# One transfer of 26 rows instead of four strided ones, when z is loaded for the last stage of an FFT convolution

## The chip, the cores and the metric

The kernel runs on one core of one Trainium2 chip. The metric is the device time of one execution in microseconds. The kernel before took 869.53 us as the median of three runs (863.26, 869.53 and 874.21). An execution by the hardware profiler took 871.26 us, of which the profile shows a span of 869.5 us.

The core has a matrix engine (TensorE, PE in the profile), three engines for element-wise work (VectorE or DVE, ScalarE or ACT, GpSimd or POOL) and SyncE (SP), which here does nothing but issue transfers. Data moves between the large memory (HBM) and the on-chip memory of 128 partitions (SBUF) by 16 DMA engines.

## The reference

The first half is a long convolution over the sequence, done by FFT; the second is a "soft mixture of experts" on its result. In short:

```python
# x: (8, 5696, 128), h: (5696, 128)
L = 2 * S
Xf = np.fft.rfft(x, n=L, axis=1)
Hf = np.fft.rfft(h, n=L, axis=0)
y = np.fft.irfft(Xf * Hf[None], n=L, axis=1)[:, :S, :]
x = y.reshape(B * S, D)                        # (45568, 128)

logits = x @ phi                               # 32 slots
d = np.exp(logits - logits.max(0));  d /= d.sum(0) + 1e-9
slot_input = (d.T @ x).reshape(8, 4, 128)
slot_out[e] = np.maximum(slot_input[e] @ w1[e], 0) @ w2[e]
c = np.exp(logits - logits.max(1, keepdims=True));  c /= c.sum(1, keepdims=True) + 1e-9
out = c @ slot_out
```

Everything is float32. All 8 batches pass through the convolution before the experts can run, since the softmax `d` goes over all 45,568 tokens.

## The kernel before

The convolution is a transform of length 5760 = 90 x 64 (`N1, N2 = 90, 64`), written as matrix products in stages. Between the stages the data goes through HBM, because the next stage needs it in another order:

- `load_x` (line 195) loads x into three buffers `xc`; `fold` (line 206, GpSimd) folds them; `first_low` and `first_high` (line 217, TensorE) do the transform over 89 rows, ScalarE copies the result out (line 220), and line 226 writes it to HBM as `f`.
- `load_g` (line 253) loads `f` into four buffers `gt`; `stage_b1` (lines 267 to 294) transforms over the 64 columns and multiplies by the filter; `stage_b2` (lines 309 to 318) transforms back and writes `z` to HBM.
- `load_pair` (line 346) loads a "pair" of column groups of `z` for all 90 rows; `stage_c1` (line 365) does the last transform over the 90 rows, lines 370 to 384 fold the result, and `stage_c2` to `stage_c6` and `dispatch` do logits, softmax terms and the sums for the slots.

There are 32 pairs, four for each batch. One step t of the main loop runs all stages for different parts of the data: the first stage of one piece, the middle of one a few steps older, the last of one older still. The order within a step is written out as two strings, `ORDER_O` and `ORDER_E`, one letter for each piece of work; a pair takes one step of each kind. `z`, the letter for `load_pair`, stands first in `ORDER_O`, and `1`, for `stage_c1`, stands in `ORDER_E`. Each engine runs its own instructions in the order in which they were written; nothing is reordered later.

SP issues nearly all transfers, in that order: about 32 for one pair. Every one of them uses one of eight completion semaphores, in turn, and waits before its issue until the transfer that used this semaphore last has landed; so no more than eight are on their way. It waits as well for the engine that makes its data or frees its buffer.

`load_pair` has one buffer `zc` (in the tail, after line 641, a second one, `zd`). It has 128 partitions of 16 KB; a row of the load, that is one of the 90 row numbers, fills one partition, 16 KB in one piece in HBM as well. Which row goes to which partition is said by `z_blocks` (lines 18 to 21), a list of (first row, rows, first partition, step of the partitions):

```python
left = [(64 + 8 * j, min(8, n - 64 - 8 * j), j, 4) for j in range((n - 57) // 8)]
return [(0, 64, 32, 1)] + left
```

For n = 90 these are rows 0 to 63 in partitions 32 to 95; rows 64 to 71 in partitions 0, 4, ..., 28; rows 72 to 79 in 1, 5, ..., 29; rows 80 to 87 in 2, 6, ..., 30; rows 88 and 89 in 3 and 7. Each entry is one transfer. Partitions 11, 15, 19, 23, 27 and 31, and those from 96 on, hold zeros. The table `i1` of the last transform, which line 365 multiplies with, is laid out by the same list, so that each row meets its own coefficients.

The tail begins after the main loop. There `zd` is taken into use and gets the six partitions of zeros below 96 by a copy from `zc` (line 653); with `zd` the matmuls read 96 partitions only (`used`).

Of the kernel before, what the change touches and what calls it, by code (L numbers as in the profile page):

```python
# [16 lines left out]

def z_blocks(n):

    left = [(64 + 8 * j, min(8, n - 64 - 8 * j), j, 4) for j in range((n - 57) // 8)]  # L20
    return [(0, 64, 32, 1)] + left


def transform_tables(S, N1, N2, CH, X0):
# [29 lines left out]
    for r, n, p, step in z_blocks(N1):  # L54
        i1[p:p + (n - 1) * step + 1:step, :, 0:NP] = part[r:r + n]
# [22 lines left out]
def kernel(  # L78
# [31 lines left out]
    N1, N2 = 90, 64  # L110
# [227 lines left out]
    def load_pair(T):  # L338
        if T >= NT:
            return  # L340
        b, j = divmod(T, NQ)
        t_ = zring.pop(0)
        zring.append(t_)
        w_ = 2 * 2 * CH * 2 * D
        for r, n, p, step in z_blocks(N1):
            nc.sync.dma_start(
                out=t_[p:p + (n - 1) * step + 1:step, :, :, :, :, :].rearrange("k h o n c d -> k (h o n c d)"),
                in_=zd[b].rearrange("q (a r) c d -> (q a) (r c d)",
                                    a=2)[r:r + n, j * w_:(j + 1) * w_])
        zs[T] = t_  # L350
# [293 lines left out]

    T = V + 1
    used = sum(z_blocks(N1)[0][1:3])
    held = slice(N1 // 64 * 8 + 3, used - 64, 4)
    front.close()
    rings.append(mid.enter_context(tc.tile_pool(name="ps2", bufs=4, space=PSUM)))
    last = work.enter_context(tc.tile_pool(name="last", bufs=1))  # L650
# [200 lines left out]
```

## Time and profile before

| | |
|---|---|
| median of three runs | 869.53 us |
| the profiled execution | 871.26 us |
| its span | 869.5 us |
| TensorE busy | 778.0 us, 89% |
| VectorE busy | 617.7 us, 71% |
| ScalarE busy | 438.1 us, 50% |
| GpSimd busy | 392.7 us, 45% |
| moved by the DMA engines | 272.01 MB, 313 GB/s on average |
| SP's transfers (queue q1) | 89.9% of 16 engines' span |
| mean granted TensorE clock | 0.939 |

"Busy" is the time in which an engine executed something. The page of the profile also follows back the chain of work that ended last, lists the groups of instructions with what ended the idle time before them, and lists the transfers by the line that issued them. Other views give the busy time in chosen stretches, the instructions in order of time, and who waited for whom. "SPq" is SP's queue of transfers; its entries say when a transfer was issued, not when it landed. The 4-byte packets in the DMA records are the writes to semaphores by which the DMA engines report that their share of a transfer is done.

### The profile page before, as it was taken

What the parts mean: (1) busy time and instruction counts of PE and PEld (TensorE: products, weight loads), DVE (VectorE), ACT (ScalarE), POOL (GpSimd) and SP (SyncE); (2) the same over time, 40 slices, a digit from 0 to 9 for tenths busy, and PEclk for the clock granted to TensorE, in tenths of its full rate; (3) what the DMA queues carried; (4) which work ended last, traced back from release to release, by engine and by line L of the source; (5) the groups of instructions that cost most, each with busy time, mean ns of one, the idle gap of its engine ahead of it and who ended that gap; (6) DMA issues with size and microseconds to landing.
All of it is one profiled execution on the core that took longest, in us unless ns stands there. A gap on an engine that the chain in (4) does not pass through costs nothing.

```text
span 869.5 us, 20507 instructions
## 1 busy us (share of the span) xinstructions
PE 778.0 (89%) x7796; PEld 378.0 (43%) x7796; DVE 617.7 (71%) x929; ACT 438.1 (50%) x967; POOL 392.7 (45%) x372
## 2 busy tenths in 40 slices
PE   5888788889999999999999999899987878978882
PEld 1122333234444444444444444444444544445882
DVE  3059867667778878887888777677888994963641
ACT  2433244354656566566556565555654444562541
POOL 4453433244565666666555556546444332541000
PEclk9999999999999999999999999999999897997755
DMA  9899899999999999999999999999988885760998
GB/s 300 267 293 320 291 332 349 326 347 330 334 320 351 334 339 331 338 350 321 328 343 341 327 329 338 329 326 342 332 279 279 319 311 206 270 263 3 371 381 325
DMA packets 153245, 272.01 MB, mean 313 GB/s; under 512 B 11878, under 2 KB 110054, under 8 KB 150005
## 3 DMA queue, kind: packets, MB, share of 16 engines
q1 hardware_dynamic: 152571, 270.38, 89.9%
q8 instruction: 63, 1.03, 0.5%
q10 hardware_dynamic: 576, 0.31, 0.1%
q14 instruction: 35, 0.29, 0.1%
HBM read 142.57 MB, written 127.98 MB: 311 GB/s over the span
## 4 chain that ended last, share of the span: by engine, by line
PE 62%; DVE 13%; DMA 12%; issue 3%; SPq 2%; ACT 1%; POOL 0%; DVEq 0%; ACTq 0%
PE bank L217 14%; PE bank L365 13%; PE bank L309 8%; PE bt L267 7%; PE bank L393 6%; DMA out_dram<-o 4%; DMA zc<-z 3%; PE bank L480 3%; DVE p L285 3%; DVE bt L285 3%; DVE yf L294 2%; PE bank L402 2%; PE bank L431 2%; DMA xc<-in_x_dram 2%; DMA gt<-f 2%
## 5 line engine op out<-in xcount | busy, mean ns | idle before, releaser
L206 POOL TENSOR_TENSOR x<-xc 128x512 f32<-128x512 f32 x144 | 180.0, 1273 | 229.8 <-PE bank L217 208.8
L217 PE MATMUL bank<-x,s 128*32 128x512 f32 (+1 forms) x1152 | 228.2, 614 | 15.5 <-POOL x L206 14.3
L315 ACT ACTIVATE zst<-bank 128x512 f32<-128x512 f32 (+1 forms) x184 | 98.6, 586 | 186.1 <-PE bank L309 165.5
L220 ACT ACTIVATE fst<-bank 128x512 f32<-128x512 f32 x216 | 127.5, 598 | 109.9 <-PE bank L217 90.3
L285 DVE TENSOR_TENSOR p<-bt,Hi 128x1024 f32<-128x1024 f32 x96 | 111.4, 1160 | 33.7 <-PE bt L267 32.9
L365 PE MATMUL bank<-zc,i 128*64 128x512 f32 x480 | 120.2, 624 | 9.2 <-DMA zc<-z 8.6
L309 PE MATMUL bank<-yf,vt 64*64 64x256 f32 x1440 | 102.9, 393 | 27.4 <-DVE yf L294 27.4
L217 PEld LDWEIGHTS bank<-x,s 128*32 128x32 f32 (+1 forms) x1152 | 56.5, 125 | 155.1 <-issue 75.8
L294 DVE TENSOR_TENSOR yf<-bt,p 128x512 f32<-128x512 f32 x192 | 119.4, 663 | 3.3
L267 PE MATMUL bt<-gt,wt 64*64 64x256 f32 x1620 | 113.7, 388 | 6.3 <-PE bt L267 2.3
L285 DVE TENSOR_TENSOR bt<-bt,Hr 128x1024 f32<-128x1024 f32 x96 | 113.0, 1177 | 0.0
L267 PEld LDWEIGHTS bt<-gt,wt 64*64 64x64 f32 x1620 | 54.0, 132 | 81.2 <-issue 38.3
L309 PEld LDWEIGHTS bank<-yf,vt 64*64 64x64 f32 x1440 | 57.0, 136 | 59.0 <-issue 31.0
L384 POOL TENSOR_TENSOR y<-y,op 128x512 f32<-128x512 f32 x64 | 77.9, 1218 | 8.7 <-DVE op L370 5.3
L370 DVE TENSOR_TENSOR y<-bank,y 128x512 f32<-128x512 f32 x32 | 22.1, 692 | 74.5 <-PE bank L365 74.2
L384 POOL TENSOR_TENSOR y<-y,om 128x512 f32<-128x512 f32 x54 | 64.0, 1185 | 2.1
L393 PE MATMUL bank<-ident,y 109*128 109x109 f32 x512 | 64.0, 277 | 0.7 <-DVE y L384 0.7
L365 PEld LDWEIGHTS bank<-zc,i 128*64 128x64 f32 x480 | 30.8, 139 | 73.3 <-issue 50.4
L393 PEld LDWEIGHTS bank<-ident,y 109*128 109x128 f32 x512 | 54.0, 150 | 16.6 <-issue 11.1
L395 ACT ACTIVATE yt<-bank 128x360 f32<-128x360 f32 x128 | 51.3, 490 | 2.9 <-PE bank L393 2.6
L804 PE MATMUL op<-so,cT 32*128 32x128 f32 x704 | 45.7, 379 | 6.0 <-ACT o L813 5.5
L439 POOL MEMSET dt<- 64x8 f32 x32 | 3.4, 106 | 101.4 <-issue 61.4
(95 smaller groups left out, 809.9 us busy)
## 6 DMA issues: line engine op xcount, KB each, us to landing
gt<-f SPq DMA_DIRECT2D x99, 512.0 KB
z<-zst SPq DMA_DIRECT2D x88, 512.0 KB
f<-fst SPq DMA_DIRECT2D x144, 240.0 KB
zc<-z SPq DMA_DIRECT2D x30, 1024.0 KB
xc<-in_x_dram SPq DMA_DIRECT2D x64, 320.0 KB
f<-fst SPq DMA_DIRECT2D x144, 120.0 KB
out_dram<-o SPq DMA_DIRECT2D x16, 1024.0 KB
zc<-z SPq DMA_DIRECT2D x90, 128.0 KB
```

The lines of the kernel that those rows point to most:

```text
L206: nc.gpsimd.tensor_tensor(out=y_[:, :, :], in0=t_[:, 0, :, :], in1=t_[:, 1, ::-1, :], op=AL.subtract if comp else AL.add)
L217: nc.tensor.matmul(p[o * width:(o + 1) * width, :], s1[:, comp + G, k], folded[(c, comp)][:, :, :].rearrange("p n d -> p (n d)"), start=Tr ...
L220: nc.scalar.activation(st[:, :, G, :], p[:, :].rearrange("p (n d) -> p n d", d=D), AF.Copy)
L267: nc.tensor.matmul(bt[q * HP:(q + 1) * HP, a, o, :], wt[r, 2 * i + q, :], t_[r, 2 * o + q, :, :].rearrange("p c d -> p (c d)"), start=True ...
L285: nc.vector.tensor_tensor(out=p_, in0=pv, in1=h_, op=AL.mult)
L294: eng.tensor_tensor(out=y_[r, 0:k, c, :], in0=pv[:, :, c, :], in1=pi[r, 0:k, 1 - c, :], op=op_)
L309: nc.tensor.matmul(bz[q][a * HP:(a + 1) * HP, o * 2 * D:(o + 1) * 2 * D], vt[r, i, a, :], y_[r, a * m + o, :, :].rearrange("p c d -> p (c ...
L315: nc.scalar.activation(st[:, 0:m, q, :], bz[q][:, 0:m * 2 * D].rearrange("p (o x) -> p o x", o=m), AF.Copy)
L365: nc.tensor.matmul(p[h_ * HP:(h_ + 1) * HP, :], i1[0:kr, tab, :], t_[0:kr, h_, o, :, q, :], start=True, stop=True)
L384: eng.tensor_tensor(out=part_, in0=part(v, 0), in1=o_[:, :, :], op=sign)
L393: nc.tensor.transpose(p[:, i * TR:(i + 1) * TR], ys[T][0:TR, k * CH + i, 0:D], ident[0:TR, 0:TR])
L395: nc.scalar.activation(yt[:, k * CH:(k + 1) * CH, :, :], of_tokens(p), AF.Copy)
```

## The change

Rows 64 to 89 come in a single transfer into partitions 0 to 25 instead of in four transfers into every fourth partition. The table `i1` follows by itself, and the partitions of zeros are now 26 to 31.

```diff
 def z_blocks(n):
 
-    left = [(64 + 8 * j, min(8, n - 64 - 8 * j), j, 4) for j in range((n - 57) // 8)]
-    return [(0, 64, 32, 1)] + left
+    return [(0, 64, 32, 1), (64, n - 64, 0, 1)]
...
     T = V + 1
     used = sum(z_blocks(N1)[0][1:3])
-    held = slice(N1 // 64 * 8 + 3, used - 64, 4)
+    held = slice(N1 - 64, used - 64)
```

`load_pair`, which loops over this list, stays as it is:

```python
for r, n, p, step in z_blocks(N1):
    nc.sync.dma_start(
        out=t_[p:p + (n - 1) * step + 1:step, ...].rearrange("k h o n c d -> k (h o n c d)"),
        in_=zd[b].rearrange(...)[r:r + n, j * w_:(j + 1) * w_])
```

So a load has two transfers, of 1 MB and 416 KB, in place of five. The bytes, their places in HBM and the matmuls that read them are the same.

## The prediction

> **What bounds the kernel now.** I read the page first, then the busy time by stretch, the DMA queue's timeline and waits, and last the DMA packet records.
>
> The page's chain of waits, one group of matmuls (busy us, mean ns, idle before and its releaser), and its DMA issues:
>
> ```profile
> PE 62%; DVE 13%; DMA 12%; issue 3%; SPq 2%; ACT 1%; POOL 0%; DVEq 0%; ACTq 0%
> ...
> L365 PE MATMUL bank<-zc,i 128*64 128x512 f32 x480 | 120.2, 624 | 9.2 <-DMA zc<-z 8.6
> ...
> zc<-z SPq DMA_DIRECT2D x30, 1024.0 KB
> ...
> zc<-z SPq DMA_DIRECT2D x90, 128.0 KB
> ...
> zc<-z SPq DMA_DIRECT2D x30, 32.0 KB
> ```
>
> TensorE carries the chain, but the only thing that the matmuls reading zc ever visibly waited for is the transfer that the change touches: 8.6 us over the run. The last three lines are that load: per pair T one transfer of 64 rows, three of 8 and one of 2, a row being 16 KB.
>
> Busy time by stretch (us busy and count per engine, granted clock, DMA share, GB/s):
>
> ```profile
> 180.00:260.00 80.00, 77.05 (x768) 34.55 (x764) 61.61 (x92) 45.00 (x96) 44.43 (x41) 0.98 0.97 334
> ...
> 340.00:420.00 80.00, 79.27 (x822) 36.92 (x820) 64.94 (x100) 48.01 (x110) 46.50 (x45) 1.00 0.97 336
> ...
> 500.00:580.00 80.00, 76.43 (x772) 35.94 (x768) 60.14 (x94) 45.93 (x106) 47.31 (x44) 0.98 0.97 332
> ...
> 720.00:780.00 60.00, 53.18 (x445) 28.78 (x444) 42.29 (x75) 33.33 (x89) 26.35 (x31) 0.89 0.70 264
> ```
>
> From 180 to 640 us two resources are full at once: PE 79.27 of 80 us, and the 16 DMA engines 0.97. In the chain the same matmuls return every 20.26 us (L217 at 335.17, 355.43, 375.69), which is one pair. From 720 us on the DMA share is 0.70.
>
> The DMA queue over half a pair, and its waits between 260 and 640 us (total us, times, longest):
>
> ```profile
> 329.11 0.35 SPq L318 DMA_DIRECT2D z<-zst  x1
> 329.56 3.23 SPq L346 DMA_DIRECT2D zc<-z  x5
> 332.84 1.50 SPq L253 DMA_DIRECT2D gt<-f  x3
> 335.09 0.82 SPq L195 DMA_DIRECT2D xc<-in_x_dram  x2
> 336.02 0.78 SPq L226 DMA_DIRECT2D f<-fst  x2
> ...
> SPq L195 <- DMA gt<-f: 35.9, 25, 2.0
> SPq L195 <- DMA zc<-z: 19.2, 23, 2.5
> SPq L226 <- DMA z<-zst: 16.7, 24, 1.0
> SPq L318 <- DMA gt<-f: 16.3, 17, 1.9
> ```
>
> SP mostly waits for earlier transfers: [...]SP is held by how fast transfers finish, not by its own issue time.
>
> The packet records of the trace, those of 16,384 bytes (only zc's rows have them in numbers), give the load itself. A packet takes 611 ns at its median in the quiet rounds (608 at least). In the load issued at 329.56 the 64-row transfer runs from 330.9 to about 334.1 as four rounds of 16; then come rounds of 8, 8, 8 and 2 that start near 334.1, 334.7, 335.3 and 336.0; the last ends at 336.71. TensorE first reads it at 338.82: 2.1 us to spare. Over the 27 loads of the main loop up to 690 us this spare time is 0.55 to 3.75 us; in ten it is under 0.9 us, and 0.55 to 0.63 is the least there is. There the landing itself released TensorE.
>
> [...] So 64 rows use 16 engines, 8 use 8, 2 use 2, and 26 will use 13. [...] q1 has 11,558 packets of 4 bytes. The rounds of 8 agree too.
>
> [...] Here a lone packet runs at 16,384 B / 611 ns = 26.8 GB/s[...].
>
> [...]
>
> **The change part by part.**
>
> *Issue.* 32 loads (30 into zc, 2 into the second buffer zd) issue 2 transfers in place of 5: 96 fewer of 0.602 us (median of L346), 58 us of SP time, 1.8 us a load. It is hidden work: SP waits on transfers behind it (L195 alone 35.9 + 19.2 us in 19 pairs, about 2.9 us a pair). What follows (the three gt transfers, xc, f) may wait for an older transfer than before, since three places of the ring of eight fall away. I take 0; at best it is worth part of C and D below.
>
> *Engines.* Before, the 26 rows cost engines 0 and 1 four packets (2.44 us), 2 to 7 three (1.83), 8 to 15 none. After, 13 engines take two each. [...] Lower bound, no mutual hindrance: 2 x 0.611 = 1.22 us, landing 1.2 us earlier. Upper bound, shared halves: [...] 2.44 us, the landing as before, but with 13 engines held for 2.44 us where 26 packets' worth of work is done. I take the upper one[...]. Added engine time: 26 x 0.611 = 15.9 us a load.
>
> *What of it reaches the end.* A pair has 16 x 20.26 = 324 us of engine time, and the share of 0.97 leaves 0.03 x 324 = 9.7 free. The overflow is 15.9 - 9.7 = 6.2 us, over 16 engines 0.39 us a pair. Through the 23 pairs from 180 to 640 us: 8.9 us. Later loads (share 0.84, then 0.70) have room: 0. The spare time before TensorE absorbs it at first but doesn't refill, as SP, the landing and TensorE go round together. Next late are the zc landing, then gt behind it[...].
>
> *Waits.* On the first load of a batch the last z rows must have landed. Before, only the 2-row transfer waited for that, at the end; now the 26-row one does, second, with gt, xc and f behind it on SP. The z transfer is issued 0.45 us before the load, so this can hold SP about 2 us, eight times; but the 64-row transfer occupies the engines for 3.2 us meanwhile. I take 0, at most 8 us.
>
> *Once.* The copy of the six zero rows into the second buffer (L653, issued at 724.15) goes from six spread partitions to 26 to 31[...]. 0. The reordered rows of the table i1 and the same 128-row matmuls cost nothing: the other engines' instructions stay as they are.
>
> Sum: + 8.9 us. The profiled execution took 871.26 us (span 869.5), 1.7 over the median of 869.53; on the median that is **878 us**.
>
> **The rivals.**
>
> A, as above: 878, from 872 (half the overflow fits elsewhere) to 886.
>
> B, slower by over 2%: the DMA engines have nothing free. 0.97 is a mean that counts overlapped packets, and a transfer is done only when its slowest engine is. Then the whole 15.9 / 16 = 0.99 us a load comes through in 30 loads: 869.5 + 30 = 899. For it: the spare time runs down inside the loop (1.83, 1.29, 1.42, 0.55, 0.86, 0.63, 0.55 in the loads issued from 411 to 533 us), so the transfers fall behind TensorE already. Against it: that time recovers after 575 us, and the tail has room. It decides once a load lands more than about 0.9 us later, which is what ten loads have at most.
>
> C, no cost: the landing is set by the four packets of engine 0 before[...]; a transfer waits for its slowest engine anyway, so engines 8 to 12 merely lose idle time. SP's 1.8 us a load helps a little: 863 to 871, say 868.
>
> D, faster: [...] loads land 1.2 us earlier, and the ten loads without spare time save about 1.1 each: 869.5 - 11 = 858. Over 2% (17 us) would need the transfers to bound most pairs, which PE at 79 of 80 us speaks against.
>
> That the change doesn't do what it says is ruled out by the built program: 26-row transfers, 96 DMAs fewer.
>
> **How the numbers follow.** A 0.36, B 0.32, C 0.24, D 0.08. About 2% is what a measurement of this kernel can tell from no change: 852 and 887 are the bounds. Slower by over 2%: B and the top of A, 0.36. Faster: the end of D, 0.04. The rest 0.60. The range is from 861 (just under C, leaving out most of D) to 902 (B with its waits).
>
> **What would show it.** Right: q1's 4-byte packets fall to 11,142; zc's last 26 packets take about 1.2 us each rather than 0.61, and the landing comes no earlier after the issue (7 to 9 us now); the DMA share rises above 0.97; L365 waits longer than 8.6 us for zc. B: the same with over 25 us of such waits or pairs of over 21 us. C: long packets, yet pairs of 20.26 us. D: packets of 0.61 us and landings 1.2 us earlier. A changed time outside 168 to 770 us would prove the whole account wrong.

## The result, and the profile after

The changed kernel takes 902.98 us as the median of four runs (900.52 to 905.14), the kernel before 868.38 us beside it (863.26 to 874.21): a ratio of 1.0388, 95% interval 1.0338 to 1.0438. It is slower by 34.6 us, clearly more than the 2% of the prediction's bound, and 1 us above the upper end of its range (861 to 902).

The page after gives the chain of waits, and the group of matmuls that reads zc (busy us, mean ns, idle before it and who ended it):

```profile
PE 49%; DMA 28%; DVE 11%; issue 3%; ACT 1%; SPq 1%; POOL 1%; DVEq 0%; ACTq 0%
PE bank L364 13%; DMA zc<-z 13%; PE bank L216 10%; PE bank L308 6%; PE bt L266 6%; DMA out_dram<-o 5%; PE bank L392 4%; DMA gt<-f 4%; DMA xc<-in_x_dram 4%; DVE p L284 2%; DVE bt L284 2%; DVE yf L293 2%; PE bank L479 2%; PE bank L430 2%; DMA f<-fst 2%
...
L364 PE MATMUL bank<-zc,i 128*64 128x512 f32 x480 | 128.9, 662 | 34.2 <-DMA zc<-z 28.6
```

The line numbers are one lower than before. Part of the chain has moved from TensorE (62% before, 49% now) to the DMA engines (12% before, 28% now). The group waits 34.2 us where it waited 9.2, and its matmuls themselves take 128.9 us in place of 120.2. Together that is 25.0 + 8.7 = 33.7 us, close to the 32.3 by which the profiled span grew (869.5 to 901.8).

The busy time of the main loop, first before and then after (us, five engines busy, granted clock, DMA share, GB/s):

```profile
260.00:640.00 380.00, 373.20 (x3838) 174.48 (x3840) 303.69 (x465) 225.62 (x516) 219.09 (x204) 1.00 0.97 334
```

```profile
260.00:640.00 380.00, 362.01 (x3608) 165.14 (x3600) 286.55 (x441) 215.39 (x489) 208.90 (x194) 0.98 1.01 317
```

The DMA engines are busier, 1.01 against 0.97, and yet move less, 317 GB/s against 334. A share above 1 also says that the records of one engine overlap, so the share isn't a fraction of something that ends at 1.

The DMA queue after, in a stretch like that shown of before, and its longest waits between 260 and 640 us (total us, times, longest):

```profile
342.62 0.35 SPq L317 DMA_DIRECT2D z<-zst  x1
343.06 2.59 SPq L345 DMA_DIRECT2D zc<-z  x2
345.71 1.48 SPq L252 DMA_DIRECT2D gt<-f  x3
347.27 1.09 SPq L194 DMA_DIRECT2D xc<-in_x_dram  x2
348.42 1.19 SPq L225 DMA_DIRECT2D f<-fst  x2
...
SPq L194 <- DMA gt<-f: 37.7, 27, 2.6
SPq L317 <- DMA zc<-z: 33.4, 18, 3.0
SPq L225 <- DMA z<-zst: 23.3, 31, 1.2
SPq L317 <- DMA gt<-f: 21.4, 18, 2.2
SPq L225 <- DMA zc<-z: 12.3, 12, 2.1
```

A load is two issues now, and in this stretch SP is through with it only a little earlier (2.59 us in place of 3.23). What it saves it loses further on: the transfers that come eight places after the load's wait 33.4 + 12.3 = 45.7 us for it, 26.0 before (19.2 + 5.4 + 1.4). In the records of after, 744 of 745 of SP's transfers use the semaphore of the one eight places before, and each is issued after that one's last write to it. (SP issues fewer transfers than the description of the kernel says: 92 from 340 to 420 us before, which is 23 for a pair and not 32.)

The starts of the zc matmuls, load by load, tell where the time went: the first is 2.5 us late (178.74 against 176.25), the 17th 27.4 us (528.24 against 500.81), the 23rd 27.5 (654.16 against 626.67), the 27th 32.8 (733.03 against 700.20). What comes after adds nothing. Between the 17th and the 23rd load nothing is lost either: there the kernel before itself took 21.0 us a pair.

In the packet records zc's 16,384-byte packets between 168 and 690 us have a mean of 852 ns (714 before), and 906 of them took over 800 ns (436 before). The packets of the 64 rows hardly changed (median 646 ns, 644 before); those of the 26 rows have a median of 1,188 ns (611 before). From the start of its first packet to the end of its last, a load takes 7.21 us on average (6.36 before). q1 has 11,142 packets of 4 bytes, 416 fewer than the 11,558 of before. That is 13 for each of 32 loads: 8 + 8 + 8 + 2 = 26 writes before, 13 after, read as 13 engines with two rows each. The records don't name the engine of a packet; engine numbers, as in the recorded texts, are the author's labels, read from rounds such as those of 8, 8, 8 and 2.

### The profile page after: what moved, and what is told of

It is laid out like the page before. It is cut to its first block, busy times and chain, and to the rows that moved or that the text cites. A ratio compares the mean times of both kernels' runs of the same rounds, so it can differ in the third digit from the quotient of the medians.

```text
span 901.8 us, 20351 instructions
## 1 busy us (share of the span) xinstructions
PE 784.9 (87%) x7796; PEld 379.0 (42%) x7796; DVE 617.6 (68%) x929; ACT 437.7 (49%) x967; POOL 392.6 (44%) x372
## 4 chain that ended last, share of the span: by engine, by line
PE 49%; DMA 28%; DVE 11%; issue 3%; ACT 1%; SPq 1%; POOL 1%; DVEq 0%; ACTq 0%
PE bank L364 13%; DMA zc<-z 13%; PE bank L216 10%; PE bank L308 6%; PE bt L266 6%; DMA out_dram<-o 5%; PE bank L392 4%; DMA gt<-f 4%; DMA xc<-in_x_dram 4%; DVE p L284 2%; DVE bt L284 2%; DVE yf L293 2%; PE bank L479 2%; PE bank L430 2%; DMA f<-fst 2%
## 5 line engine op out<-in xcount | busy, mean ns | idle before, releaser
L364 PE MATMUL bank<-zc,i 128*64 128x512 f32 x480 | 128.9, 662 | 34.2 <-DMA zc<-z 28.6
L364 PEld LDWEIGHTS bank<-zc,i 128*64 128x64 f32 x480 | 33.7, 147 | 101.8 <-issue 72.5
```

Source lines behind the costliest of these rows:

```text
L364: nc.tensor.matmul(p[h_ * HP:(h_ + 1) * HP, :], i1[0:kr, tab, :], t_[0:kr, h_, o, :, q, :], start=True, stop=True)
```

## The experiments

Theory P is the author's assumption behind the upper bound of the prediction, which no view of before showed: engines that write at the same time to partitions close together (neighbours, or every second one) halve each other, called sharing below; an engine that takes four neighbouring partitions by itself is not held up. Two rivals stood against it: S, that the number of transfers and the ring of eight semaphores matter, and W, that the 26 rows now wait for z's last rows. Each kernel's ratio is to the kernel before on the same chip. The diffs show the lines that matter; "..." stands for further lines.

**The loads by themselves.** Only the loads are left, on idle DMA engines.

```diff
+def load(r, n, p, step):
+    nc.sync.dma_start(out=t[p:p + (n - 1) * step + 1:step, :], in_=rows[r:r + n, 0:4096])
...
```

> Nothing of the computation is left: only loads of 16 KB rows into one cleared buffer, one after the other on idle DMA engines, each form twice: 1 row; 8 rows on every fourth partition, on every second, on neighbours; 26 rows on neighbours; 28 rows on neighbours but four to one engine; then whole loads as before (64, 8, 8, 8, 2), as after (64, 26) and as 64 + 28. Theory P[...]: packets of 0.61, 1.22 and 2.44 us for 8 rows on every fourth, every second and neighbouring partitions; 1.22 us each for the 26 rows, 2.44 us in all; 0.61 us each for the 28 rows, also 2.44 us in all. The three whole loads then last the same to 0.3 us. Rival S (it is the number of transfers and the ring of eight semaphores) and rival W (it is the wait for z's last rows): 0.61 us for every packet, and 1.2 us for the 26 rows.

From its packet records (16,384-byte packets; each form twice):

```
form                                   first to last, us   packets, ns
8 rows, every 4th partition            1.20  1.20          608 to 1133
8 rows, every 2nd                      1.16  1.17          608 to 1153
8 rows, neighbours                     1.63  1.50          794 to 1522
26 rows, neighbours, 13 engines        2.64  2.61          738 to 1309, the later 13 of the 1st load 859 to 1240
28 rows, 4 to an engine, 7 engines     3.16  3.39          first row 946 to 1511, the others 611
64, 8, 8, 8, 2 (before)                5.46  5.66
64, 26 (after)                         5.29  5.46
64, 28                                 5.75  5.79
```

An engine's first packet takes between 0.6 and 1.5 us in any form, which hides the sharing in the forms of one row to an engine; the clean steps of 0.61, 1.22 and 2.44 us that I expected for 8 rows are not there, and the 28 rows take 3.2 to 3.4 us in place of 2.44. The later rows show the sharing: 611 ns in the 28 rows, with four neighbouring partitions to an engine, 859 to 1,240 ns in the later 13 of the first load of 26, with two to an engine. None of the 26 packets came down to 611 ns. The other half of the finding is in the last lines: by itself, the load after is no longer than the load before, rather 0.2 us shorter. That holds for idle DMA engines only; in the full kernel the load after is longer (7.21 us against 6.36, above).

**Five transfers, but on every second partition.**

```diff
-    left = [(64 + 8 * j, min(8, n - 64 - 8 * j), j, 4) for j in range((n - 57) // 8)]
+    left = [(64, 8, 0, 2), (72, 8, 1, 2), (80, 8, 16, 2), (88, n - 88, 17, 2)]
...
```

> The kernel before, with its five transfers of 64, 8, 8, 8 and 2 rows, but each of the small ones on every second partition[...]. Theory P: each round of 8 takes 1.22 us in place of 0.61, the landing comes up to 2.4 us later, and with no spare time the whole run takes 895 to 945 us. Rivals S and W: nothing that they speak of is changed, 868 us within 6.

944.51 us, ratio 1.0810 (1.0723 to 1.0898). The number of transfers, the number of engines used (11,558 packets of 4 bytes on q1, as before) and the waits are those of before; only the partitions differ. The matmuls that read zc, and the main loop:

```profile
L365 PE MATMUL bank<-zc,i 128*64 128x512 f32 x480 | 137.3, 699 | 68.5 <-DMA zc<-z 54.1
```

```profile
260.00:640.00 380.00, 345.32 (x3426) 158.90 (x3426) 269.17 (x414) 202.49 (x463) 195.75 (x181) 0.97 0.97 299
```

The idle time before these matmuls is 68.5 us, and the packets after the 64 rows have a median of 1,072 ns. The DMA share is 0.97 as before, at 299 GB/s in place of 334: a loss for this reason doesn't need a higher share. An estimate from the rounds of 8, 8, 8 and 2: if each packet takes 0.61 us more, the two engines with four rows get the most, 2.44 us; times 30 loads that is 73 us, and 71 were lost by the ratio. S and W fall for this kernel. It is the cleanest of the tests, since nothing but the destination partitions was changed.

**Two transfers, but four neighbouring partitions to one engine.**

```diff
+    return [(0, 64, 32, 1), (62, 28, 0, 1)]
...
+            if n == 28:
+                src = src.rearrange("(i e) x -> e i x", e=7)
...
```

> The kernel after, with two transfers, 64 rows and 28 (rows 62 and 63 come a second time, and their second copy meets coefficients of zero), where the source is ordered so that seven engines take four rows each[...]. Theory P: packets of 0.61 us, no sharing, 862 to 874 us, level with before. Rivals S and W: still two transfers, the second still waits for z's last rows, so 897 to 909 us, as after.

874.77 us, ratio 1.0040 (1.0007 to 1.0073), 0.8 us above the range for theory P and far below that of the rivals. Its later packets are at 612 ns again (median). Its q1 has 10,948 packets of 4 bytes, 11,142 - 10,948 = 194 fewer than after: 32 x 6 for a split over 7 engines in place of 13, and 2 because the copy of zeros has 4 rows in place of 6.

```profile
L369 PE MATMUL bank<-zc,i 128*64 128x512 f32 x480 | 120.4, 624 | 18.0 <-DMA zc<-z 15.8
```

**Its twin, in the natural order.** The same 28 rows without the reordering of the source, hence 14 engines with two rows each.

```diff
-            if n == 28:
-                src = src.rearrange("(i e) x -> e i x", e=7)
```

> The twin of the 64 + 28 kernel: the same two transfers with the same bytes, partitions and waits, but with the source in its natural order, so that 14 engines take two rows each[...]. Theory P: 28 packets of about 1.2 us again, 897 to 912 us. If what made the 64 + 28 kernel level with before was its two doubled rows or anything but the order of the rows: 868 to 882 us, as that one.

905.81 us, ratio 1.0428 (1.0366 to 1.0491).

```profile
L367 PE MATMUL bank<-zc,i 128*64 128x512 f32 x480 | 130.3, 668 | 44.5 <-DMA zc<-z 36.2
```

The twin has the slow matmuls and the long waits of the kernel after, the kernel above has not. Both have the same two transfers, bytes, partitions and waits. What differs is which rows an engine gets, and that alone is 31 us. The median of the later packets is 1,199 ns, 612 in the kernel above. The order of the rows makes two changes at once: 14 engines in place of 7 (the page counts 11,492 packets under 512 bytes, 11,268 in the kernel above, 224 = 32 x 7 more), and sharing in place of none. These two kernels don't part them, but the five transfers above do: the number of engines stayed the same there.

**Without the wait of 26 rows.**

```diff
+    return [(0, 64, 32, 1), (64, 24, 0, 1), (88, n - 88, 24, 1)]
```

> The kernel after, with the 26 rows on the same neighbouring partitions but as 24 rows and 2, so that only the last 2 have to wait for z's last rows. Theory P: [...] 895 to 909 us. Rival W: the wait of 26 rows is gone, 885 us or less. Rival S: one more transfer in the ring, a third of the way back, about 891 us.

912.13 us, ratio 1.0481 (1.0407 to 1.0555). Nothing comes back, so W is not the cause. It is 3 us above the range expected for theory P; why it may even be slower than after (the intervals overlap) stays open.

**More engine time, no sharing.**

```diff
+        nc.sync.dma_start(
+            out=t_[96:125:4, :, :, :, :, :].rearrange("k h o n c d -> k (h o n c d)"),
+            in_=zd[b].rearrange(...)[64:72, j * w_:(j + 1) * w_])
```

> The kernel before with one transfer more for each load: rows 64 to 71 come a second time, to partitions 96, 100, ..., 124[...], on engines 0 to 7; they meet coefficients of zero. [...] If the end is set by engine time as a mean over 16 engines: 8 x 0.61 / 16 = 0.31 us a load, 30 loads, 877 us. If by the engine that has most to do: 0.61 us a load, 886 to 889 us. If the loads have spare time (a load's length doesn't matter): 871 within 4.

898.07 us, ratio 1.0370 (1.0296 to 1.0444): 29.4 us, or 0.98 us for each of 30 loads, more than all three forecasts. A load of eight more rows costs nearly as much as the change does, without longer packets (median of the later ones 619 ns):

```profile
L369 PE MATMUL bank<-zc,i 128*64 128x512 f32 x480 | 126.7, 652 | 35.2 <-DMA zc<-z 29.0
```

Whether the packets or the additional transfer do it was asked next.

**One more transfer without engine time.** 512 bytes in place of the eight rows.

```diff
+        nc.sync.dma_start(
+            out=t_[127:128, 0, 0, 0, 0, :],
+            in_=zd[b][0:1, 0, 0, :])
```

> The kernel before with one more transfer for each load, of 512 bytes to a partition that meets coefficients of zero: a place in the ring of eight and an issue on SP, but no engine time. If the 29 us of the kernel with eight more rows came from its additional transfer: 885 us or more. If they came from its eight packets on engines 0 to 7: 869 within 5.

869.77 us, ratio 1.0005 (0.9981 to 1.0030). One more place in the ring and an issue of 0.418 us (median) on SP cost nothing that can be measured. With the 64 + 28 kernel, which has two transfers and is nearly level with before, S is out.

**The two rows filled up to eight.**

```diff
-    left = [(64 + 8 * j, min(8, n - 64 - 8 * j), j, 4) for j in range((n - 57) // 8)]
+    left = [(64 + 8 * j, 8, j, 4) for j in range(3)] + [(82, 8, 3, 4)]
...
```

> The kernel before with its last transfer of 2 rows grown to 8 (rows 82 to 87 come a second time and meet coefficients of zero): still five transfers[...], six more packets on engines 2 to 7, which then have four like engines 0 and 1. If the engine with most to do counts: no change, 869 within 4. If the mean over 16 engines counts: 6 x 0.61 / 16 x 30 = 7 us more, 876. If every engine that has to do more delays the rest, as with eight more rows: some 20 us more, 885 to 892. (The one copy of six zero rows in the tail is left out, since no zeros are left there.)

881.36 us, ratio 1.0119 (1.0091 to 1.0147), 11.1 us, between the second and the third forecast. The engines with most to do keep their four packets, and still it costs, so not they alone count; and it is more than the mean over 16 engines gives (7 us).

**Before and after with room on the DMA engines.** In both, three quarters of the loads of x are left out.

```diff
+        if c >= 3 and c % 4:
+            xs[c] = t_
+            return
```

> The kernel before without three quarters of the loads of x after the third (the folds read what stands in the buffers, so the result is not that of the reference): about 8% fewer bytes, engine work unchanged, DMA share about 0.9. TensorE then sets the pairs at 20.2 us: 845 to 870 us.

> The kernel after with the same three quarters of the loads of x left out. If the sharing costs time because it takes engine time from DMA engines that are full: with 8% free (26 us of engine time a pair against 15.9 added) it costs little, at most 10 us more than the kernel before so lightened. If each load simply lands about 1.1 us later and TensorE waits for it: 30 to 35 us more, as at full load.

854.68 us (ratio 0.9847, 0.9791 to 0.9903) and 857.05 us (0.9876, 0.9813 to 0.9939): with the same sharing the change costs 2.4 us by the medians instead of 34.6. That is within the spread of the runs (851.86 to 857.45 and 852.92 to 861.68); the two profiled executions are 6.4 us apart (855.24 and 861.68). The matmuls that read zc, in the lightened kernel before, then in the lightened one after:

```profile
L368 PE MATMUL bank<-zc,i 128*64 128x512 f32 x480 | 117.5, 612 | 1.0 <-issue 0.6
```

```profile
L367 PE MATMUL bank<-zc,i 128*64 128x512 f32 x480 | 120.2, 624 | 12.7 <-DMA zc<-z 10.1
```

The main loop, in the same order:

```profile
260.00:640.00 380.00, 374.56 (x3860) 175.84 (x3860) 307.13 (x473) 227.10 (x519) 218.06 (x203) 1.00 0.90 311
```

```profile
260.00:640.00 380.00, 373.21 (x3853) 174.56 (x3854) 306.18 (x473) 225.42 (x517) 216.76 (x202) 1.00 0.95 310
```

The bytes are equal, 311 and 310 GB/s, and the share rises by 0.05. Of 324 us of engine time for a pair that is about 16 us over all transfers; zc's later packets themselves account for 26 x (1,048 - 643 ns) = 10.5 us of it (means). So the sharing takes engine time in either case, and here it cost little.

That the DMA engines had time to give is one reading of this pair. There is another, which it doesn't exclude: with fewer loads of x the loads of zc also had more spare time. From the landing to the first matmul that reads zc it is 4.1 us on average in the lightened kernel before, 1.5 us in the kernel before at full load.

**What a load lasts in each kernel.** The packet records of the same runs, for the loads issued between 165 and 695 us (24 to 27 in each): from the start of a load's first 16,384-byte packet to the end of its last (mean, with a standard error of 0.1 to 0.25 us), the packets after those of the first 64 rows (median), and the time lost in the whole run divided by 30 loads.

```
kernel                           first to last, us   later packets, ns   lost a load, us
before                           6.36                 611
one more transfer of 512 bytes   6.31                 611                0.0
64 + 28, four rows to an engine  6.66                 612                0.1
two rows filled up to eight      6.68                 611                0.4
64 + 28, natural order           7.14                1,199               1.2
after                            7.21                1,188               1.2
eight more rows                  7.29                 619                1.0
64 + 24 + 2                      7.47                1,154               1.4
five transfers, every 2nd        8.55                1,072               2.4
lightened before                 5.91                 611
lightened after                  6.25                1,134               0.1
```

At full load the loss goes with what a load lasts longer, whatever makes it longer: 0.85 us longer and 1.2 lost after, 0.93 and 1.0 with eight more rows, 2.19 and 2.4 with five transfers on every second partition. In the lightened pair a load lasts only 0.34 us longer, and there is spare time to take that up. This is agreement over nine kernels at full load, not an experiment on the length alone.

## Why the prediction was wrong

The packets got as long as the prediction took them to be; what of it reaches the end was taken at less than a third of what it is. Point by point:

- *Engines.* Right for 13 engines (416 fewer packets of 4 bytes, 13 a load) and for the upper bound of a packet: about 1.2 us (median 1,188 ns). That packets which share take twice as long was an estimate that nothing in the profile of before showed; the sum of 15.9 us applied it to all 26. In the full kernel zc's later packets took 26 x (1,112 - 640 ns) = 12.3 us more a load (means).
- *What of it reaches the end.* **This is the step that failed.** It took the share of 0.97 as 9.7 us free for each pair, let those absorb most of the 15.9, and passed 0.39 us on. Measured: 34.6 us over 30 loads, 1.15 us each. In its place the runs show that the free 0.03 was no room: the kernels with 6 and 8 packets more have 3.7 and 4.9 us of engine time more (6 and 8 x 0.61), well under 9.7, and lost 11 and 29 us. Nor is the mean over 16 engines the measure: for eight packets it gives 0.31 us a load, and 0.98 were lost. What the loss goes with is the length of the load itself (table above). Why the added packets make a load so much longer stays open; the records don't name the engine of a packet.
- *The landing.* "As before" belongs to the same step. It is right for a lone load (5.3 to 5.5 us against 5.5 to 5.7) and wrong in the full kernel, where a load lasts 0.85 us longer. The prediction had said that it decides once a load lands more than about 0.9 us later, since ten loads have no more to spare; its sum then took the landing as unchanged.
- *Rival B.* Its 899 comes near the 903, but by the mean over 16 engines (0.99 us a load), which the kernel with eight more rows contradicts. That it came so near was in part luck.
- *A cost that the sum didn't have.* After a wait for a late load the next matmuls can run at half clock. In the timeline after (start, us, engine, idle before and its releaser), and in the two stretches around it (PE clock third from the end):

```profile
325.13 3.79 PE L216 MATMUL bank<-x,s 128*64 128x512 f32 x24
332.11 3.49 PE L364 MATMUL bank<-zc,i 128*64 128x512 f32 x8 [3.19 <-DMA zc<-z]
...
336.12 1.94 PE L364 MATMUL bank<-zc,i 128*64 128x512 f32 x8
```

```profile
332.10:335.60 3.50, 3.49 (x9) 0.90 (x10) 0.00 (x0) 0.60 (x1) 0.00 (x0) 0.54 1.11 305
336.10:338.10 2.00, 2.00 (x13) 0.60 (x16) 1.58 (x3) 1.68 (x4) 0.34 (x2) 1.00 1.03 387
```

  Eight matmuls take 3.49 us after a wait of 3.19, and 1.94 us four microseconds later. The granted clock is 0.50 from 331.87 to 335.29, 3.4 us; it fell 2.95 us after the last matmul's end (328.92). Between 160 and 690 us TensorE had 27.3 us at half clock after against 17.1 before, and its busy time in the whole run grew by 6.9 us (778.0 to 784.9). How much of the 34.6 us this is, the runs don't show.
- *The spare time doesn't refill.* Right in its outcome: from the first load to the 17th the delay grew from 2.5 to 27.4 us, 1.6 us a load. The time from the landing to the first matmul didn't shrink, though: 1.57 us on average after, 1.54 before. TensorE came as much later as the loads did.
- *Later loads have room: 0.* Half right. From the 23rd load to the 27th (654 to 733 us) another 5.3 us were lost; after that nothing.
- *Issue.* Right: 96 transfers fewer gained nothing that could be seen (64 + 28 rows: not faster than before), and 32 more, of 512 bytes, cost nothing.
- *Waits.* Right to take 0: 24 + 2 rows gave nothing back. *Once* (the copy of zeros) wasn't tried alone.
- The range missed by 1 us; its upper end stood for B with its waits.

No kernel here beats the one before. Of those with two transfers, 64 + 28 rows with four neighbouring partitions to an engine comes nearest, 3.8 us behind it.

## What to carry to other kernels

Ask of a transfer not only how large it is and how many there are, but which of its rows an engine carries and how close together the partitions are that several engines write to at once: reordering the source rows of one transfer, with the same bytes and the same destination, was worth 31 us here, and every second partition in place of every fourth cost 71. When a DMA share stands near 1, as here at 0.97, don't count the rest as room: 3.7 us of engine time more a pair, of 9.7 that seemed free, already cost 11 us. Ask how much longer the load itself lasts and whether the engine that waits for it has that much to spare; at a share of 0.90 and with 4.1 us to spare the same sharing cost 2.4 us, which is within the spread of the runs. Read the GB/s beside the share: it fell after (317 of 334, share 1.01) and with five transfers on every second partition (299, share 0.97 as before).

## What the runs showed of the hardware that was not expected

- One lone load of 26 rows with two rows to an engine lasts 2.6 us, against 3.2 to 3.4 for 28 rows with four to an engine, while two rows to an engine cost 31 to 35 us in a kernel at a DMA share of 0.97.
- The same five transfers on the same number of engines, with the small ones on every second partition instead of every fourth, made the whole kernel 8% slower.
- Eight packets more for each load, at 619 ns each, cost 0.98 us a load; a transfer more with 512 bytes cost nothing that can be measured (ratio 1.0005).
- After a wait of 3.19 us for a transfer eight matmuls took 3.49 us, at a granted clock of 0.54, in place of 1.94 at full clock.
